# Another order for scores and weighted values in the steps that carry no block of projections

## The chip, the cores and the metric

The kernel runs on one core of one Trainium2 chip. The metric is the device time of one launch in microseconds (us). A figure for "before" is the median of its timed runs; a profile comes from one further execution, whose own time is given beside it.

## What is computed

Two attention blocks, A and B, run over the same 2048 tokens of 640 features, with 32 heads of 20 features each and with weights of their own. A sigmoid gate mixes their outputs token by token. Cut to what matters:

```
def block(x, wqkv, wo):                       # x: 1 x 2048 x 640
    q, k, v = split(x @ wqkv)                 # 32 heads, Dh = 20
    p = softmax(q @ k.T * Dh ** -0.5)         # full 2048 x 2048, each head
    return (p @ v) @ wo

g = sigmoid((x * gate_w).sum(-1, keepdims=True))
return g * block(x, A_wqkv, A_wo) + (1 - g) * block(x, B_wqkv, B_wo)
```

## The kernel before

Four heads form a group, and each block has eight groups, so there are 16 in all (`2 * NG`). For each group the kernel walks over four blocks of 512 queries, and for each of these over eight pairs of key tiles of 128 keys. One such pair, for one query block and four heads, is a *step*: 16 x 4 x 8 = 512 steps (`STEPS`). A step `G` issues three kinds of TensorE work:

- eight **e** matmuls (line 672, in `scores`): scores of 128 keys against 512 queries for one head. ScalarE turns each into exponentials (line 675) and stores them in a buffer `pt`.
- up to eight **m** matmuls (line 614, in `max_mm`): scores of 128 queries against 512 keys for a later step's softmax maximum, some 15 steps ahead. Most are reduced on VectorE by one maximum (line 625). One in eight, in the groups of which this text speaks, goes to ScalarE instead (a ReLU, line 618), and VectorE joins it with another matmul's scores (line 622). So a full step gives ScalarE eight exponentials and one ReLU, and VectorE six maxima and one joined maximum.
- two **V**, the blocks of weighted values (line 690, in `values`): for 128 keys, four matmuls with the exponentials of four heads, which add into the tile `acc`. They use the exponentials of step `G - 1`.

An e or m matmul uses one half of TensorE's rows: heads with `j = 0` the partitions from 0 on, heads with `j = 1` those from 64 on. In the strings below, `e0` and `m0` stand for the first half, `e1` and `m1` for the second. Both kinds are called *scores* in this text. Each writes one of seven PSUM tiles (`bank`, `NB = 7`), and the tile is free again when ScalarE or VectorE has read it. `take` hands out the tiles while the program is written, by a running estimate of which comes free first. `acc` has a tile of its own.

Beside this the steps carry other TensorE work: *blocks*, written **X**, are pieces of the next groups' projections or of the output product (line 407). The function `slot` issues one. The rest of the step (DMAs, small tasks) is advanced once for each `e`.

The order in which a step's pieces are issued is written out by hand, in three strings, one for steps without a block, one for steps with one, and one for steps with two. Cut to its core, the loop is:

```
STEP = ("e0 m1 V e1 m0 e0 m1 e1 m0 e0 m1 e1 m0 V e0 m1 e1 m0",
        "X e0 m1 m0 e1 m0 m1 V m1 e0 e1 m0 e1 e0 V m0 e1 e0 m1",
        "X m0 m1 e0 m1 e0 e1 V e1 e0 m1 m0 V e1 m0 m1 m0 e0 e1 X")
...
        blocks = 0 if not current and not any(f[0] <= G for f in fill) else 2 if behind(G) else 1
        for what in (STEP[blocks] if maxima or some else ...).split():
            k = count[what] = count.get(what, 0) + 1
            if what[0] == "e":   # also: advance the small tasks
                scores(G, (k - 1) // 2, (k - 1) % 2, (int(what[1]),))
            elif what[0] == "m":
                for u, ch in some[(k - 1) * len(some) // 4:k * len(some) // 4]:
                    one_max(u, ch, int(what[1]))
            elif what == "V":
                values(G - 1, k - 1)
            else:
                slot(G)
```

TensorE, ScalarE and VectorE each take their instructions in the order of the program.

`STEP[0]` is used in 20 of the 512 steps: 60 to 65, 162 to 167, 184 and 185, 190 and 191, and the single steps 452, 459, 466 and 489. All 20 have their full eight m. The steps with one block are by far the most. In the text, V1 and V2 are the two V of a step, and *inner* is a pair of neighbouring steps that both use `STEP[0]`.

Of the kernel before, what the change touches and what calls it, by code (L numbers as in the profile page):

```python
# [50 lines left out]
OFINE = (16, 16, 6, 16)  # L51


STEP = ("e0 m1 V e1 m0 e0 m1 e1 m0 e0 m1 e1 m0 V e0 m1 e1 m0",
        "X e0 m1 m0 e1 m0 m1 V m1 e0 e1 m0 e1 e0 V m0 e1 e0 m1",
        "X m0 m1 e0 m1 e0 e1 V e1 e0 m1 m0 V e1 m0 m1 m0 e0 e1 X")
LATE = "e0 e1 e0 e1 V X e0 e1 e0 e1 V"
# [14 lines left out]
def kernel(  # L72
# [1100 lines left out]
    for G in range(STEPS + 1):  # L1173
# [12 lines left out]
        count = {}  # L1186
        for what in (STEP[blocks] if maxima or some else LATE + " X" * (blocks == 2)).split():
            k = count[what] = count.get(what, 0) + 1
# [58 lines left out]
```

## Time and profile before

| | |
|---|---|
| median of 3 runs | 2762.35 us (2762.08 to 2764.07) |
| the profiled execution's own time | 2762.97 us |
| its span, first to last instruction | 2761.2 us |
| granted TensorE clock, mean | 0.996 |
| PE (TensorE matmul) busy | 2722.8 us, 99% of the span |
| ACT (ScalarE) busy | 2528.5 us, 92% |
| DVE (VectorE) busy | 2444.3 us, 89% |
| POOL (GpSimd) busy | 667.0 us, 24% |

The views name an engine, a line of the kernel and the tiles (`out<-in`), with the count behind an x. In the view in order of time, a row gives start and length in us, and equal neighbours are merged into one row with their count. A V shows there as one row of eight matmuls, since each of its four shows twice. A busy share is that of an engine's spans, and the ends of matmuls are modelled, so that short waits of PE can lie hidden under it.

### The profile page before, as it was taken

To read this page: it belongs to the slowest core of one execution; us is meant where nothing else is said; L and a number is where in the kernel's file an instruction comes from. 1 tells how busy PE (TensorE), PEld (TensorE's weight loads), DVE (VectorE), ACT (ScalarE), POOL (GpSimd) and SP (SyncE) were. 2 spreads that over 40 slices of the span, in tenths; PEclk is the share of its full clock that TensorE was granted. 3 is DMA by queue.
4 is the path that set the end of the run, shared out by engine and by line. 5 is a ranking of instruction groups with operands and counts; after the bars stand their busy time and mean duration, and the time that the engine had idled before them with its cause. 6 is when DMAs were issued, how large, how long until landed. Compare 5 with 4: busy or idle time off the path is not lost.

```text
span 2761.2 us, 62247 instructions
## 1 busy us (share of the span) xinstructions
PE 2722.8 (99%) x23273; PEld 935.9 (34%) x23273; DVE 2444.3 (89%) x4785; ACT 2528.5 (92%) x5128; POOL 667.0 (24%) x909
## 2 busy tenths in 40 slices
PE   7999999999999999999999999999999999999998
PEld 3433333333333332333333333333333333333222
DVE  7789899999999989888888998989988898999982
ACT  4999999999999999999999999999999999999987
POOL 6232222222123421311221111222342202100111
PEclk8999999999999999999999999999999999999999
DMA  4021102010120211102012230221201112132112
GB/s 143 16 57 26 31 11 47 7 31 16 25 55 20 60 42 49 43 9 61 20 45 62 60 85 25 60 56 48 65 17 42 30 50 63 32 78 63 47 48 76
DMA packets 176432, 125.58 MB, mean 45 GB/s; under 512 B 105216, under 2 KB 145976, under 8 KB 176128
## 3 DMA queue, kind: packets, MB, share of 16 engines
q1 hardware_dynamic: 173584, 119.99, 17.1%
q8 instruction: 182, 2.98, 0.5%
q0 software_dynamic: 1600, 0.96, 0.2%
q14 instruction: 122, 1.00, 0.1%
q10 hardware_dynamic: 944, 0.66, 0.1%
HBM read 55.53 MB, written 31.86 MB: 32 GB/s over the span
## 4 chain that ended last, share of the span: by engine, by line
PE 94%; DVE 4%; ACT 1%; DMA 1%; issue 0%; POOL 0%; POOLq 0%; SPq 0%; ACTq 0%; DVEq 0%
PE acc L690 35%; PE bank L407 20%; PE bank L614 20%; PE bank L672 18%; DVE mpart L625 2%; ACT pt L675 1%; DMA ws<-in_A_wqkv_dram 0%; PE bank L854 0%; DVE rl L622 0%; PE bank L900 0%; DVE ot L777 0%; DMA xs<-in_A_x_dram 0%; POOL wstage L336 0%; ACT rl L618 0%; DVE es L216 0%
## 5 line engine op out<-in xcount | busy, mean ns | idle before, releaser
L675 ACT ACTIVATE pt<-bank 128x512 f32<-128x512 f32 x4096 | 2168.5, 613 | 146.0 <-PE bank L672 98.0
L625 DVE TENSOR_REDUCE mpart<-bank 128x1 f32<-128x512 f32 x2944 | 1843.7, 682 | 220.4 <-PE bank L614 118.8
L690 PE MATMUL acc<-pt,v 128*21 128x512 f32 x8192 | 1081.7, 600 | 1.4 <-DVE ot L777 1.2
L672 PE MATMUL bank<-qt,kt 64*128 64x512 f16 x4096 | 1041.7, 380 | 4.6 <-DVE mpart L625 2.9
L614 PE MATMUL bank<-kt,qt 60*128 60x512 f16 x3520 | 1011.6, 380 | 4.2 <-ACT pt L675 1.3
L614 PEld LDWEIGHTS <-qt 60*128 60x128 f16 x4096 | 238.4, 94 | 883.4 <-issue 821.9
L622 DVE CUSTOM_DVE_ANT_0 rl<-bank,rl 128x512 f32<-128x512 f32 x576 | 388.1, 680 | 7.0 <-ACT rl L618 2.2
L618 ACT ACTIVATE rl<-bank 128x512 f32<-128x512 f32 x576 | 336.9, 594 | 7.1 <-PE bank L614 6.7
L672 PEld LDWEIGHTS <-kt 64*128 64x128 f16 x4096 | 230.2, 94 | 199.4 <-issue 88.5
L690 PEld LDWEIGHTS acc<-pt,v 128*21 128x21 f32 x8192 | 143.0, 99 | 431.9 <-issue 426.4
L407 PE MATMUL bank<-xx,wbh 128*128 128x168 f16 (+3 forms) x2480 | 287.7, 236 | 1.4 <-DVE wbh L926 1.0
L407 PE MATMUL bank<-xx,wbl 128*128 128x168 f16 (+3 forms) x1240 | 257.5, 235 | 0.0
L785 POOL TENSOR_TENSOR ot<-ot,sq 128x512 f32<-128x512 f32 x63 | 66.0, 1048 | 755.3 <-DVE sq L782 755.3
L407 PEld LDWEIGHTS <-wbh 128*128 128x128 f16 x2480 | 192.8, 98 | 110.8 <-issue 104.5
L614 PE MATMUL bank<-kd,qt 60*128 60x512 f16 x576 | 203.7, 379 | 0.1
L407 PE MATMUL bank<-woh,o_in 128*128 128x320 f16 (+3 forms) x700 | 157.7, 290 | 0.0
L407 PE MATMUL bank<-wvh,xx 128*128 128x160 f16 (+1 forms) x1280 | 156.7, 234 | 0.6 <-DVE mpart L622 0.6
L436 POOL CAST cq<-fs 128x512 f16<-128x512 f32 x60 | 36.6, 610 | 477.3 <-ACT fs L434 473.6
L407 PEld LDWEIGHTS <-xx 128*128 128x128 f16 x1920 | 131.1, 97 | 59.1 <-issue 56.3
L407 PE MATMUL bank<-wvl,xx 128*128 128x160 f16 (+1 forms) x640 | 137.7, 232 | 0.0
L407 PEld LDWEIGHTS <-wbl 128*128 128x128 f16 x1240 | 121.1, 98 | 4.7 <-issue 1.3
L407 PEld LDWEIGHTS <-o_in 128*128 128x128 f16 (+1 forms) x1050 | 87.3, 97 | 90.7 <-issue 68.8
(145 smaller groups left out, 1247.4 us busy)
## 6 DMA issues: line engine op xcount, KB each, us to landing
y_scr<-y_out SPq DMA_DIRECT2D x48, 320.0 KB
y_out<-y_scr SPq DMA_DIRECT2D x32, 320.0 KB
kt<-cq SPq DMA_DIRECT2D x120, 80.0 KB
o_scr<-on SPq DMA_DIRECT2D x240, 40.0 KB
o_in<-o_scr SPq DMA_DIRECT2D x64, 96.0 KB
kt<-cq SPq DMA_DIRECT2D x136, 40.0 KB
wstage<-in_B_wqkv_dram SPq DMA_DIRECT2D x13, 400.0 KB
xs<-in_A_x_dram SPq DMA_DIRECT2D x8, 640.0 KB
```

What stands on the lines that cost most here:

```text
L407: nc.tensor.matmul(out_ap, a, b, start=(k == 0), stop=(k == len(pairs) - 1))
L436: nc.gpsimd.tensor_copy(hi, f)
L614: nc.tensor.matmul(pt, QT[g % 2][r, pair, q0:q0 + P], k, start=True, stop=True)
L618: nc.scalar.activation(relus[u, j], pt, AF.Relu)
L622: nc.vector.tensor_tensor_reduce(rl, pt, rl, 1.0, LOW, OP.add, OP.max, m)
L625: nc.vector.tensor_reduce(m, pt, axis=AX.X, op=OP.max)
L672: nc.tensor.matmul(et, KT[g % 2][r, pair, kt * P:(kt + 1) * P], QT[g % 2][r, pair, qb * QB:(qb + 1) * QB], start=True, stop=True)
L675: nc.scalar.activation(pt, et, AF.Exp, scale=factor(g // 4))
L690: nc.tensor.matmul(acc[32 * h:32 * h + VW, :], V[(g // 2) % 2][:, kt, (g % 2) * GH + h, :], ptiles.pop((G, kk, h)), start=(kt == 0), stop= ...
L785: nc.gpsimd.tensor_tensor(t3, t3, sq.unsqueeze(2).to_broadcast([P, 16, 32]), op=OP.mult)
```

## The change

Only the first string changes. It holds the same pieces in the same numbers (four each of e0, e1, m0 and m1, and two V).

```
-STEP = ("e0 m1 V e1 m0 e0 m1 e1 m0 e0 m1 e1 m0 V e0 m1 e1 m0",
+STEP = ("e0 m0 m1 V m0 e1 e1 m0 m1 e1 e0 V e0 m1 m1 e0 e1 m0",
         "X e0 m1 m0 e1 m0 m1 V m1 e0 e1 m0 e1 e0 V m0 e1 e0 m1",
```

The instructions of PE, DVE and ACT are moved within the 20 steps, and from the first of them on the scores' PSUM tiles carry other numbers. Apart from those numbers, nothing else in the order of these three engines differs, and on POOL and SP the order is the same throughout.

First place: PE, the beginning of step 60, from its first e to just behind its first V. L672 is an e, L614 an m (`kd` and `kt` are keys, `qt` queries), and the row of L690 is the V. Before:

```order
L672 LDWEIGHTS kt_83
L672 MATMUL bank_90<-qt_81,kt_83 128x512
L614 LDWEIGHTS qt_80
L614 MATMUL bank_89<-kt_82,qt_80 128x512
L690 MATMUL acc<-pt,v_86 21x512 x4
L672 LDWEIGHTS kt_83
L672 MATMUL bank_93<-qt_81,kt_83 128x512
```

The same place in the changed kernel:

```order
L672 LDWEIGHTS kt_83
L672 MATMUL bank_90<-qt_81,kt_83 128x512
L614 LDWEIGHTS qt_80
L614 MATMUL bank_89<-kd_84,qt_80 128x512
L614 LDWEIGHTS qt_80
L614 MATMUL bank_93<-kt_82,qt_80 128x512
L690 MATMUL acc<-pt,v_86 21x512 x4
L614 LDWEIGHTS qt_80
L614 MATMUL bank_94<-kt_82,qt_80 128x512
```

One more score stands ahead of V1: the m on `kd`, which came behind it before. Of the three, the first two are e0 and m0, on the same half of the rows.

Second place: ACT, the nine instructions of step 60, eight exponentials (L675) and one ReLU (L618). Before:

```order
L675 ACTIVATE pt<-bank_90 128x512
L675 ACTIVATE pt<-bank_93 128x512
L618 ACTIVATE rl<-bank_94 128x512
L675 ACTIVATE pt<-bank_91 128x512
L675 ACTIVATE pt<-bank_95 128x512
L675 ACTIVATE pt<-bank_89 128x512
L675 ACTIVATE pt<-bank_92 128x512
L675 ACTIVATE pt<-bank_90 128x512
L675 ACTIVATE pt<-bank_95 128x512
```

And in the changed kernel:

```order
L675 ACTIVATE pt<-bank_90 128x512
L618 ACTIVATE rl<-bank_89 128x512
L675 ACTIVATE pt<-bank_91 128x512
L675 ACTIVATE pt<-bank_92 128x512
L675 ACTIVATE pt<-bank_93 128x512
L675 ACTIVATE pt<-bank_89 128x512
L675 ACTIVATE pt<-bank_91 128x512
L675 ACTIVATE pt<-bank_95 128x512
L675 ACTIVATE pt<-bank_93 128x512
```

The ReLU comes one place earlier. Before, one of these nine belongs to a score ahead of V1, six to scores between V1 and V2, and two to scores behind V2; now it is two, four and three.

## The prediction

> **What bounds the kernel now.** I read the page's busy table and its chain first, then one run of six neighbouring steps with the first string as a whole, then PE in order of time inside that run. The busy table and the chain, shares of the span:
>
> ```profile
> PE 2722.8 (99%) x23273; PEld 935.9 (34%) x23273; DVE 2444.3 (89%) x4785; ACT 2528.5 (92%) x5128; POOL 667.0 (24%) x909
> ...
> PE 94%; DVE 4%; ACT 1%; DMA 1%; issue 0%; POOL 0%; POOLq 0%; SPq 0%; ACTq 0%; DVEq 0%
> ```
>
> By these, TensorE is all that counts. But the change touches 20 steps of 512, so they must be read by themselves. The six steps 162 to 167 lie between 921 and 954 us; the view by windows gives the busy time of PE, PEld, DVE, ACT and POOL there:
>
> ```profile
> 921.00:954.00 33.00, 32.10 (x234) 7.95 (x231) 31.07 (x60) 31.42 (x63) 18.42 (x20) 1.00 0.29 62
> ```
>
> Here ACT is busy for 95% of the time and DVE for 94%, more than over the whole kernel, and PE for 97%. Three engines are close to full, so what counts is who waits for whom. PE in order of time, from the V2 of step 164 (937.82) over the V1 of step 165 (939.56) to its V2 (942.41):
>
> ```profile
> 937.82 1.05 PE L690 MATMUL acc<-pt,v 128*21 128x512 f32 x8
> 938.81 0.39 PE L672 MATMUL bank<-qt,kt 64*128 64x512 f16 x1
> 938.81 0.60 PE L614 MATMUL bank<-kt,qt 60*128 60x512 f16 x2
> 939.04 0.59 PE L672 MATMUL bank<-qt,kt 64*128 64x512 f16 x2
> 939.26 0.38 PE L614 MATMUL bank<-kt,qt 60*128 60x512 f16 x1
> 939.56 1.05 PE L690 MATMUL acc<-pt,v 128*21 128x512 f32 x8
> 940.55 0.39 PE L672 MATMUL bank<-qt,kt 64*128 64x512 f16 x1
> 940.55 0.39 PE L614 MATMUL bank<-kd,qt 60*128 60x512 f16 x1
> 940.78 0.38 PE L614 MATMUL bank<-kt,qt 60*128 60x512 f16 x1
> 940.78 0.59 PE L672 MATMUL bank<-qt,kt 64*128 64x512 f16 x2
> 941.00 0.38 PE L614 MATMUL bank<-kt,qt 60*128 60x512 f16 x1
> 941.22 0.38 PE L672 MATMUL bank<-qt,kt 64*128 64x512 f16 x1
> 941.62 0.37 PE L614 MATMUL bank<-kt,qt 60*128 60x512 f16 x1
> 941.97 0.37 PE L672 MATMUL bank<-qt,kt 64*128 64x512 f16 x1
> 942.11 0.37 PE L614 MATMUL bank<-kt,qt 60*128 60x512 f16 x1
> 942.41 1.05 PE L690 MATMUL acc<-pt,v 128*21 128x512 f32 x8
> ```
>
> Four lengths can be read off. A V holds the next score back by 0.99 us (939.56 to 940.55). Two scores on different halves start together (940.55), and the next pair follows 0.22 later (940.78, 941.00, 941.22): I call 0.22 a *pitch*. A V starts 0.30 after the last score (942.11 to 942.41). And the stretch from V1 to V2, ten scores or five pitches' worth, takes 2.85 where 0.99 + 4 x 0.22 + 0.30 = 2.17 would do. Its first seven scores go at the pitch; the eighth, at 941.62, comes 0.40 after the seventh, and the rest go one by one. The other stretch, from V2 to V1 with six scores, takes 1.74 and has no wait.
>
> Why the eighth waits is seen on ACT in the same stretch:
>
> ```profile
> 940.98 0.60 ACT L675 ACTIVATE pt<-bank 128x512 f32<-128x512 f32 x1
> ...
> 941.47 0.59 ACT L618 ACTIVATE rl<-bank 128x512 f32<-128x512 f32 x1
> 941.95 0.60 ACT L675 ACTIVATE pt<-bank 128x512 f32<-128x512 f32 x1
> ```
>
> There are seven tiles for scores. The first exponential begins 0.43 after its score (940.55 to 940.98), takes 0.60 and ends at 941.58; 0.04 later, at 941.62, the eighth score starts. It has waited for this tile. Ten scores between two V are more than seven tiles carry, and six are fewer; while PE is in a V, ACT and DVE have only the left-over scores to live on.
>
> ACT's own pitch is 0.48 (941.47 to 941.95), so its nine instructions need at least 9 x 0.48 = 4.32 us a step. DVE's pitch is that of a row of four maxima with no gap inside (window on DVE):
>
> ```profile
> 1209.38 2.48 DVE L625 TENSOR_REDUCE mpart<-bank 128x1 f32<-128x512 f32 x4 [0.48 <-PE bank L614]
> ```
>
> (2.48 - 0.68) / 3 = 0.60, with the single one's 0.68 from the group below; six of them and one joined maximum, 0.68, make 4.28 us:
>
> ```profile
> L625 DVE TENSOR_REDUCE mpart<-bank 128x1 f32<-128x512 f32 x2944 | 1843.7, 682 | 220.4 <-PE bank L614 118.8
> L622 DVE CUSTOM_DVE_ANT_0 rl<-bank,rl 128x512 f32<-128x512 f32 x576 | 388.1, 680 | 7.0 <-ACT rl L618 2.2
> ```
>
> An inner step takes 1.74 + 2.85 = 4.59 now. Neither engine's floor explains that: about 0.27 a step is bad order.
>
> **The change part by part.** The new string has three scores ahead of V1, seven between V1 and V2, and six behind V2. Nothing is added or taken away, no DMA changes its place in SP's or POOL's queue, and V2 still finds its four exponentials one whole step old. So all is in three kinds of stretch.
>
> *V1 to V2, 20 times.* Seven scores fit into seven tiles. On the halves they read 0 1, 1 0, 1, 1 0: four pitches with one half-empty, so 0.99 + 3 x 0.22 + 0.30 = 1.95 us. That the first seven after a V go without a wait is what the rows from 940.55 to 941.22 show. Against 2.85 this is -0.90, times 20: **-18.0**. I cost all twenty at 2.85. The first and the last of the twenty, and the one of step 162, in order:
>
> ```profile
> 408.80 1.06 PE L690 MATMUL acc<-pt,v 128*21 128x512 f32 x8
> 411.65 1.06 PE L690 MATMUL acc<-pt,v 128*21 128x512 f32 x8
> ...
> 923.14 1.06 PE L690 MATMUL acc<-pt,v 128*21 128x512 f32 x8
> 924.88 1.06 PE L690 MATMUL acc<-pt,v 128*21 128x512 f32 x8
> 928.30 1.06 PE L690 MATMUL acc<-pt,v 128*21 128x512 f32 x8
> ...
> 2634.71 1.06 PE L690 MATMUL acc<-pt,v 128*21 128x512 f32 x8 [0.20 <-DVE ot L777]
> 2637.63 1.06 PE L690 MATMUL acc<-pt,v 128*21 128x512 f32 x8
> ```
>
> They take 2.85, 3.42 and 2.92, and all twenty together 60.4, which is 3.4 over 20 x 2.85. I take that surplus to be other VectorE work that falls into such a stretch, and leave it in: it is worth -3.4 if the freer tiles swallow it, and nothing if not.
>
> *V2 to V1, 12 times inside a run.* Now nine scores follow each other: six, then e0 m0 m1 of the next step. On the halves: 0 1, 1 0, 1 0, 0, 0 1. That is five pitches, 0.99 + 4 x 0.22 + 0.30 = 2.17 without a wait. But the eighth has to wait for a tile again. The first exponential behind V2 frees one at 0.99 + 0.43 + 0.60 + 0.04 = 2.06, later than the eighth's place at 0.99 + 0.88 = 1.87. The ninth waits for the first maximum, 0.99 + 0.43 + 0.68 + 0.04 = 2.14, and V1 comes at 2.44. Against 1.74 that is +0.70, times 12: **+8.4**. An inner step is then 1.95 + 2.44 = 4.39 instead of 4.59, just over ACT's 4.32 and DVE's 4.28, so both can follow. The ends are 2.37, which with 1.95 makes ACT's floor, and 2.85, what ten scores take now.
>
> *Into a run, 8 times.* Three scores stand ahead of V1 where there were two, and e0 and m0 share a half: one pitch, +0.22. Ahead of step 162 (923.14 to 924.88, 1.74) nothing waits today, so the floor is near; if the third score has to wait for one more exponential, it is 0.22 + 0.48 = 0.70. I take +0.30: **+2.4**.
>
> *Out of a run, 8 times.* Behind the last V2 stand six scores in place of four, +0.22, and one exponential and one maximum more are left over for the next step. That step begins with a block, which covers them in part, as at step 452, a single one:
>
> ```profile
> 2451.71 1.06 PE L690 MATMUL acc<-pt,v 128*21 128x512 f32 x8
> ...
> 2453.24 0.27 PE L407 MATMUL bank<-woh,o_in 128*128 128x216 f16 x1
> ...
> 2454.18 0.39 PE L672 MATMUL bank<-qt,kt 64*128 64x512 f16 x1
> ```
>
> The block holds PE for 0.94 (2453.24 to 2454.18), in which ACT and DVE can do one such extra each; but they are behind already when it starts. The ends are +0.22 and 0.22 + 0.60 = +0.82 (a whole maximum uncovered). I take +0.42, a third of the way, since the block covers the larger part: **+3.4**.
>
> The sum is -18.0 + 8.4 + 2.4 + 3.4 = **-3.8 us** on the profiled execution's 2762.97, which gives 2759.2. The median of the runs is 0.6 lower, so I forecast 2758.6.
>
> **A rule that speaks against it.** The string puts same-half scores beside each other (e0 m0, e1 e1 later on). The rows at 940.55 show that different halves start together, and those at 940.78 and 941.00 that one half takes a new score each 0.22. The Trainium skill, "TensorEngine Tiling (Array Packing)", Key Properties, says that different tiles of the array can load weights and multiply in parallel, which makes alternating halves the good order. By that rule alone, with TensorE as the bound, only lost pitches would count. The trace agrees with the rule, but not with the bound: 0.68 of the 2.85 is waiting, three times a pitch.
>
> **The rivals.** About 0.2%, 5.5 us, is what I take a measurement of this kernel to tell from no change.
>
> - *More gain* (chance 0.18). The surplus of 3.4 goes too, entries and exits cost their floor of 0.22 (-0.6 and -1.6), and inner steps reach ACT's 4.32 (12 x -0.07 = -0.8): -10.2, 2752.1. For it: DVE idles beside PE's waits. Against it: surplus VectorE work must be done in any case.
> - *All comes back* (0.14). ACT and DVE are at 95% and 94%, so the time gained between V1 and V2 returns as waits for tiles: 0.90 a step in each inner V2 to V1 (10.8) and 0.45 in each entry and exit (7.2): 0, 2762.4. Against it: the floors of 4.32 and 4.28 lie below 4.59.
> - *Only pitches count* (0.04). The sixteen scores take eight pitches now (1 ahead of V1, 5 between, 2 behind) and nine in the new string (2, 4 and 3), as pairs on one half share none. One pitch more, 0.22, in 20 steps with every wait as it is: +4.4, 2766.8. Against it: the waits hang on the ten scores that are gone.
> - *Slower* (0.06). Nine scores run out of tiles as the ten do today. V2 to V1 then takes 2.85 in inner steps (12 x 1.11 = 13.3), entries and exits cost their upper ends (8 x 0.70 = 5.6, 8 x 0.82 = 6.6): +7.5, 2769.9. With such entries and exits, an inner V2 to V1 over 2.68 is what makes it more than 5.5 us. For it: the stretch is only one score shorter than the one that waits now. Against it: two of its nine scores wait by the rows, not three.
>
> **How the numbers follow.** The forecast, -3.8 or thereabouts, has the remaining 0.58. It is a difference of large terms, 18.0 against 14.2, so its own ends (-5.5 to -1) come from an error of 0.1 us in an inner stretch and 0.1 in an exit. The range of 8 in 10 takes in half of the way to the larger gain and most of the case in which all comes back, and leaves out the last two rivals and the full gain: 2755.0 to 2763.0. Faster by over 0.2% is the first rival alone, 0.18; slower the last, 0.06; the forecast and the other two lie within 0.2%, 0.76.
>
> **What would show it.** In the changed profile, V1 to V2 in the run of 162 to 167 should be near 1.95 with no gap among its seven scores, V2 to V1 near 2.44 with the wait at the eighth score, and a whole inner step near 4.39. Step 452's stretch from V2 (2451.71, above) to the next V1, in the row below, is 3.22 and should grow to about 3.6:
>
> ```profile
> 2454.93 1.06 PE L690 MATMUL acc<-pt,v 128*21 128x512 f32 x8
> ```
>
> Outside the 20 steps and the one behind each, nothing should move. It would be wrong if the seven scores wait between V1 and V2, if inner V2 to V1 comes to 2.68 or more, or if steps far from the 20 change because tiles are handed out in another rotation.

## The result, and the profile after

| | before | after |
|---|---|---|
| median of 22 runs each | 2762.86 us (2762.07 to 2764.49) | 2759.18 us (2758.43 to 2761.13) |
| profiled execution's own time | 2762.97 us | 2761.0 us |
| its span | 2761.2 us | 2759.2 us |

The ratio is 0.9987, with a 95% interval of 0.9982 to 0.9993: 3.7 us or 0.13% faster. The interval leaves out 1, and the gain is within the 0.2% that the prediction counted as no change. The forecast was -3.8 us (2758.6).

PE in order of time in the changed kernel, from the V2 of step 164 (936.44) over the V1 of step 165 (938.94) to its V2 (940.90), the same place as in the prediction:

```profile
936.44 1.06 PE L690 MATMUL acc<-pt,v 128*21 128x512 f32 x8
937.43 0.39 PE L672 MATMUL bank<-qt,kt 64*128 64x512 f16 x1
937.44 0.39 PE L614 MATMUL bank<-kt,qt 60*128 60x512 f16 x1
937.66 0.38 PE L672 MATMUL bank<-qt,kt 64*128 64x512 f16 x1
937.66 0.59 PE L614 MATMUL bank<-kt,qt 60*128 60x512 f16 x2
937.88 0.59 PE L672 MATMUL bank<-qt,kt 64*128 64x512 f16 x2
938.54 0.37 PE L614 MATMUL bank<-kd,qt 60*128 60x512 f16 x1
938.63 0.37 PE L614 MATMUL bank<-kt,qt 60*128 60x512 f16 x1
938.94 1.05 PE L690 MATMUL acc<-pt,v 128*21 128x512 f32 x8
939.92 0.39 PE L614 MATMUL bank<-kt,qt 60*128 60x512 f16 x1
939.93 0.39 PE L672 MATMUL bank<-qt,kt 64*128 64x512 f16 x1
940.15 0.38 PE L614 MATMUL bank<-kt,qt 60*128 60x512 f16 x1
940.15 0.38 PE L672 MATMUL bank<-qt,kt 64*128 64x512 f16 x1
940.37 0.38 PE L614 MATMUL bank<-kt,qt 60*128 60x512 f16 x1
940.50 0.46 PE L672 MATMUL bank<-qt,kt 64*128 64x512 f16 x2
940.90 1.06 PE L690 MATMUL acc<-pt,v 128*21 128x512 f32 x8
```

V1 to V2 takes 1.96 us (2.85 before): its seven scores take no more than the four pitches that they need (the row at 940.50 joins the last two, of which the second starts at 940.59). V2 to V1 takes 2.50 (1.74 before): seven scores at the pitch, then a hole up to the eighth at 938.54. An inner step takes 4.46 where it took 4.59 (4.39 forecast). What the eighth and the ninth wait for stands on ACT and DVE. A pair of exponentials on ACT, then one maximum on DVE:

```profile
937.38 1.11 ACT L675 ACTIVATE pt<-bank 128x512 f32<-128x512 f32 x2
```

```profile
937.89 0.69 DVE L625 TENSOR_REDUCE mpart<-bank 128x1 f32<-128x512 f32 x1
```

The second of the exponentials is the one of the first score behind V2. It ends at 937.38 + 1.11 = 938.49, and the eighth score starts at 938.54; the maximum ends at 938.58, and the ninth starts at 938.63.

The run of 162 to 167 by windows, with the busy times of PE, PEld, DVE, ACT and POOL (the window ends 1 us earlier than the one before, as the run does):

```profile
921.00:953.00 32.00, 31.62 (x237) 8.72 (x237) 31.01 (x59) 31.14 (x64) 18.19 (x19) 1.00 0.30 63
```

ACT is busy for 97% of it and DVE for 97%, where it was 95% and 94%. The starts of the V in all 20 steps give the terms of the prediction's sum (sums over the steps named, from one profiled execution of each kernel):

| stretch | before | after | difference | predicted |
|---|---|---|---|---|
| V1 to V2, 20 times | 60.44 | 41.10 | -19.3 | -18.0 |
| V2 to V1 inside a run, 12 | 23.35 | 33.03 | +9.7 | +8.4 |
| into a run, 8 | 14.83 | 17.18 | +2.4 | +2.4 |
| out of a run, 8 | 27.80 | 31.27 | +3.5 | +3.4 |
| sum | 126.42 | 122.58 | -3.8 | -3.8 |

The two profiled executions differ by 2.0 us only, since the stretches before the first V, between the other steps and behind the last V are 0.4, 0.4 and 1.0 us longer in this execution of the changed kernel. The first lies ahead of every moved instruction, so it is no effect of the change, and the last is 0.1 us shorter than before in the run with alternating halves in this schedule (below), so that one varies too. In the middle part, the largest changes are +0.3, +0.2 and +0.1 us in the steps just behind a run (186, 490 and 467) and -0.3 in step 316, which is far from any. The first three look like an effect that reaches one step further than the table; with one execution of each kernel that is not shown. Its 22 runs spread over 2.7 us. The median is the measure of the whole, and the trace that of the parts.

### The profile page after: what moved, and what is told of

The parts are those of the page before. It is cut to its first block, busy times and chain, and to the rows that moved or that the text cites. A ratio compares the mean times of both kernels' runs of the same rounds, so it can differ in the third digit from the quotient of the medians.

```text
span 2759.2 us, 62203 instructions
## 1 busy us (share of the span) xinstructions
PE 2722.9 (99%) x23273; PEld 940.3 (34%) x23273; DVE 2443.9 (89%) x4785; ACT 2528.0 (92%) x5128; POOL 666.7 (24%) x909
## 4 chain that ended last, share of the span: by engine, by line
PE 94%; DVE 3%; ACT 1%; DMA 1%; issue 0%; POOL 0%; POOLq 0%; SPq 0%; ACTq 0%; DVEq 0%
PE acc L690 35%; PE bank L407 20%; PE bank L614 20%; PE bank L672 18%; DVE mpart L625 2%; ACT pt L675 1%; DMA ws<-in_A_wqkv_dram 0%; PE bank L854 0%; DVE rl L622 0%; PE bank L900 0%; DMA xs<-in_A_x_dram 0%; DVE ot L777 0%; DVE es L216 0%; ACT rl L618 0%; PE bank L829 0%
## 5 line engine op out<-in xcount | busy, mean ns | idle before, releaser
L675 ACT ACTIVATE pt<-bank 128x512 f32<-128x512 f32 x4096 | 2166.9, 613 | 143.0 <-PE bank L672 101.4
L690 PE MATMUL acc<-pt,v 128*21 128x512 f32 x8192 | 1081.9, 600 | 0.1
L672 PE MATMUL bank<-qt,kt 64*128 64x512 f16 x4096 | 1038.1, 380 | 2.4 <-DVE mpart L625 1.3
L614 PE MATMUL bank<-kt,qt 60*128 60x512 f16 x3520 | 1008.5, 381 | 4.1 <-ACT pt L675 1.5
L614 PEld LDWEIGHTS <-qt 60*128 60x128 f16 x4096 | 238.9, 94 | 900.3 <-issue 833.0
L618 ACT ACTIVATE rl<-bank 128x512 f32<-128x512 f32 x576 | 338.1, 596 | 7.4 <-PE bank L614 7.0
L672 PEld LDWEIGHTS <-kt 64*128 64x128 f16 x4096 | 230.6, 95 | 176.7 <-issue 66.5
L690 PEld LDWEIGHTS acc<-pt,v 128*21 128x21 f32 x8192 | 143.7, 99 | 431.3 <-issue 426.6
L614 PE MATMUL bank<-kd,qt 60*128 60x512 f16 x576 | 203.6, 379 | 1.3 <-DVE mpart L622 0.5
```

Of the source, the lines that this page charges most:

```text
L614: nc.tensor.matmul(pt, QT[g % 2][r, pair, q0:q0 + P], k, start=True, stop=True)
L618: nc.scalar.activation(relus[u, j], pt, AF.Relu)
L672: nc.tensor.matmul(et, KT[g % 2][r, pair, kt * P:(kt + 1) * P], QT[g % 2][r, pair, qb * QB:(qb + 1) * QB], start=True, stop=True)
L675: nc.scalar.activation(pt, et, AF.Exp, scale=factor(g // 4))
L690: nc.tensor.matmul(acc[32 * h:32 * h + VW, :], V[(g // 2) % 2][:, kt, (g % 2) * GH + h, :], ptiles.pop((G, kk, h)), start=(kt == 0), stop= ...
```

## The experiments

In the kernel's own schedule the change is worth 3.7 us, too little to tell theories apart by their size. So a schedule was made that uses the first string 13 times as often: of each eight steps, four get two blocks each and four none. In it 260 steps use the string, in 63 runs with 197 inner pairs.

**Old and new string, used 260 times.** The edit of both, and the text on record for each:

```
         blocks = 0 if not current and not any(f[0] <= G for f in fill) else 2 if behind(G) else 1
+        if blocks and G < 496:
+            blocks = 2 if G % 8 < 4 else 0
```

> The old string, in a schedule that uses it 13 times as often: of each eight steps the first four get two blocks each and the last four none, as far as there are blocks. It is then used in 260 steps, in 63 runs, with 197 inner pairs. This is the base for the others of this set. All theories: slower than the kernel before, as the four steps in a row without a block leave TensorE waiting for ScalarE and VectorE (4.59 us a step), and the two-block steps are longer than TensorE's mean; inner steps should take 4.59 as before, V1 to V2 2.85, V2 to V1 1.74.

> The same schedule with the new string. Theory (the count of scores between two V against seven PSUM tiles decides): the four terms as they were measured in the change, 260 x -0.97 (V1 to V2) + 197 x 0.81 (inner V2 to V1) + 63 x 0.30 (into a run) + 63 x 0.43 (out of a run) = -46 us against the old string in this schedule. Rival 1 (only the pitches of the halves count): 260 x 0.22 = +57 us. Rival 2 (ScalarE and VectorE are the bound, and what is gained comes back): 0 within 10 us.

Measured: 2897.16 us with the old string and 2852.83 with the new one (ratios to the kernel before 1.0485, interval 1.0467 to 1.0502, and 1.0323, 1.0306 to 1.0340). The new string is 44.3 us faster, 46 were expected; rivals 1 and 2 gave +57 and 0. A row for each V of neighbouring steps, V1 first, old string and then new:

```profile
1732.69 1.06 PE L690 MATMUL acc<-pt,v 128*21 128x512 f32 x8
1735.54 1.06 PE L690 MATMUL acc<-pt,v 128*21 128x512 f32 x8
1737.28 1.06 PE L690 MATMUL acc<-pt,v 128*21 128x512 f32 x8
```

```profile
1706.78 1.06 PE L690 MATMUL acc<-pt,v 128*21 128x512 f32 x8
1708.74 1.06 PE L690 MATMUL acc<-pt,v 128*21 128x512 f32 x8
1711.24 1.06 PE L690 MATMUL acc<-pt,v 128*21 128x512 f32 x8
```

2.85 and 1.74 against 1.96 and 2.50: to 0.01 us the stretches of the kernel's own 20 steps. By the two traces, the four kinds of stretch add up to -44.1 us (-234.1, +156.7, +14.1 and +19.2), and all the rest differs by 0.5. So the gain is one of the string and grows with its use; it doesn't come from other steps, where only the rotation of the tiles is new.

**Eight and eight.** The first string becomes the one in the text on record.

> The same schedule, with eight scores between V1 and V2 and eight between V2 and V1, halves strictly alternating (eight pitches a step, the fewest there can be): e0 m1 V e1 m0 e0 m1 e1 m0 e0 m1 V e1 m0 e0 m1 e1 m0. Theory (tiles): in both stretches the eighth score waits for the first exponential behind the V, so each takes 0.99 + 0.43 + 0.60 + 0.04 + 0.30 = 2.36 and an inner step 4.72, more than with the old string (4.59): 260 x (2.36 - 2.85) + 197 x (2.36 - 1.74) + 63 x 0.30 = +14 us against the old string in this schedule, that is about 60 us slower than the new one. Rival (an even split feeds ScalarE and VectorE best, and no pitch is lost): at least as fast as the new string, with inner steps at ScalarE's 4.32, some -55 us against the old.

Measured: 2929.69 us (1.0603, 1.0585 to 1.0621), 32.5 us slower than the old string and 77 slower than the new. The rival is refuted: the even split without a lost pitch is the slowest of the three. The theory had the sign, and less than half of the size. PE in an inner step, from a V2 (1752.48) over the next V1 (1754.93) to its V2 (1757.36):

```profile
1752.48 1.06 PE L690 MATMUL acc<-pt,v 128*21 128x512 f32 x8
1753.47 0.39 PE L672 MATMUL bank<-qt,kt 64*128 64x512 f16 x1
1753.47 0.60 PE L614 MATMUL bank<-kt,qt 60*128 60x512 f16 x2
1753.70 0.59 PE L672 MATMUL bank<-qt,kt 64*128 64x512 f16 x2
1753.92 0.38 PE L614 MATMUL bank<-kt,qt 60*128 60x512 f16 x1
1754.14 0.38 PE L672 MATMUL bank<-qt,kt 64*128 64x512 f16 x1
1754.62 0.37 PE L614 MATMUL bank<-kt,qt 60*128 60x512 f16 x1
1754.93 1.06 PE L690 MATMUL acc<-pt,v 128*21 128x512 f32 x8
...
1757.36 1.05 PE L690 MATMUL acc<-pt,v 128*21 128x512 f32 x8
```

The eighth score alone is late: it starts 1754.62 - 1752.48 = 2.14 behind the V, where 2.06 was expected. It does wait for the first exponential, as the theory has it, but this one comes later. ACT, the exponential of the score at 1753.47:

```profile
1753.96 0.62 ACT L675 ACTIVATE pt<-bank 128x512 f32<-128x512 f32 x1
```

It begins 0.49 behind its score and not 0.43, and ends at 1754.58, 0.04 ahead of the eighth score. In 438 of the 459 stretches of this run with eight scores and no block, the trace puts the end of the eighth's wait down to an exponential. Why it begins later here is open. The stretches from V1 to V2 and from V2 to V1 are then 2.43 and 2.45 here, where 2.36 was expected of both: over 260 and 197 of them that is 18 + 18 = 36 us. Half of it was taken back, as the old string's stretches in this schedule are on average 2.90 and 1.77 and not 2.85 and 1.74 (means over all 260 and 197).

**The new counts with alternating halves.** Only the order within the stretches differs from the new string.

> The same schedule, with the new string's counts (three scores ahead of V1, seven between, six behind) but with the halves alternating as far as odd counts let them: e0 m1 m0 V e1 m0 e1 e0 m1 e1 m0 V e0 m1 m0 e1 e0 m1. Theory (counts and tiles): the same as the new string, within 5 us. Rival (neighbours on the same half are a price that the new string pays): faster than the new string by up to 0.22 x 260 = 57 us.

Measured: 2851.05 us (1.0319, 1.0302 to 1.0336), 1.8 us faster than the new string in this schedule, within the 5 of the theory and far from the rival's 57. But the rival's price was set too high: seven scores take four pitches and nine take five in whichever order, so both strings have nine pitches a step, and there was no lost pitch to win back. What this run shows is that at equal pitches it hardly counts which halves are neighbours. That a lost pitch doesn't decide is shown by eight and eight, which has eight pitches a step and is 77 us slower. The same was tried in the kernel's own schedule:

> The kernel's own schedule (20 steps) with the new string's counts, three, seven and six, but halves alternating as far as they can. Theory (counts decide, not which halves are neighbours): -3.7 us against the kernel before, as the change, within 1 us. Rival (the change pays for neighbours on one half): up to 4.4 us faster than the change, about -8.

Measured: 2759.61 us against 2762.12 of the kernel before (0.9991, interval 0.9982 to 1.0000), -2.5 us. The four terms of its trace add up to -3.7 (-19.3, +9.7, +2.3 and +3.6), as the change's do to -3.8. The median misses the expected -3.7 by 1.2 us, 0.2 more than was allowed for; the intervals of the two strings overlap, and I read no difference between them. It is not the rival's -8, which rests on the same price as its 57.

**One tile fewer.** In the steps that use the first string, scores get six PSUM tiles instead of seven. Old and new string, both in the schedule with 260 uses:

```
-    now = [-1]
+    now, few = [-1], [0]
...
-        i = min((k for k in range(NB) if k not in held), key=lambda k: free_at[k])
+        i = min((k for k in range(NB - few[0]) if k not in held), key=lambda k: free_at[k])
...
-        count = {}
+        count, few[0] = {}, 1 if not blocks and maxima else 0
```

> The old string in the schedule that uses it 260 times, with one PSUM tile fewer (six) handed out to scores in just these steps. Theory (tiles decide): in the ten scores between V1 and V2 the seventh waits already, so that V1 to V2 grows from 2.85 by 0.2 to 0.4; the six scores from V2 to V1 still fit, 1.74 in inner steps. In all 50 to 110 us slower than with seven tiles. Rival (ScalarE and VectorE are the bound by their throughput, and tiles only pass the wait on): within 10 us of seven tiles.

> The same with the new string. Theory (tiles decide): seven scores no longer fit. Between V1 and V2 the seventh waits for the first exponential, 2.06 + 0.30 = 2.36 instead of 1.96; from V2 to V1 the ninth waits for the second exponential (about 0.99 + 0.43 + 0.48 + 0.63 + 0.04 = 2.57), 2.87 instead of 2.49: 260 x 0.40 + 197 x 0.38 = +180 us against seven tiles, and with six tiles the new string has lost its advantage over the old one. Rival (throughput): within 10 us of seven tiles, and still some 45 us faster than the old string.

Measured: 3010.08 us with the old string (1.0898, 1.0881 to 1.0915) and 3032.86 with the new (1.0978, 1.0961 to 1.0995). Against seven tiles that is +113 (50 to 110 expected, so a little over the range) and +180 (180 expected); the kernel before, run beside each set, took 2763.63 us beside the seven tiles and 2762.12 beside the six. The new string has not only lost its lead, it is 23 us behind. V1, V2 and the next V1 with six tiles, old string:

```profile
1804.96 1.06 PE L690 MATMUL acc<-pt,v 128*21 128x512 f32 x8
1808.27 1.06 PE L690 MATMUL acc<-pt,v 128*21 128x512 f32 x8
1810.02 1.06 PE L690 MATMUL acc<-pt,v 128*21 128x512 f32 x8
```

Its six scores still fit into six tiles, and V2 to V1 stays at 1.75; the ten wait longer, 3.31 (3.05 to 3.25 expected). The new string over one step, V1 at 1819.20:

```profile
1819.20 1.06 PE L690 MATMUL acc<-pt,v 128*21 128x512 f32 x8
...
1820.86 0.81 PE L672 MATMUL bank<-qt,kt 64*128 64x512 f16 x2
1821.60 1.06 PE L690 MATMUL acc<-pt,v 128*21 128x512 f32 x8
...
1823.73 0.37 PE L672 MATMUL bank<-qt,kt 64*128 64x512 f16 x1 [0.32 <-ACT pt L675]
1823.94 0.38 PE L614 MATMUL bank<-kd,qt 60*128 60x512 f16 x1
1824.22 0.37 PE L614 MATMUL bank<-kt,qt 60*128 60x512 f16 x1
1824.52 1.06 PE L690 MATMUL acc<-pt,v 128*21 128x512 f32 x8
```

V1 to V2 is 2.40, since the seventh score (the second in the row at 1820.86) now has to wait, and V2 to V1 is 2.92. The text on record gave 2.36 and 2.87. The row at 1823.73 is the seventh score behind V2, and names what ended its wait: an exponential. The instructions and their order per engine are those of the run with seven tiles, only the tiles' numbers differ; so the tiles are what decides here, and not the engines' throughput. The Trainium skill, "TensorEngine Tiling (Array Packing)", PSUM Bottleneck, says that tiling speeds up TensorE but not the evacuation of PSUM. These runs agree: behind a V, TensorE starts seven scores within 0.66 us when there are seven tiles, and with six the seventh starts only when a reader has freed a tile.

None of these runs points to an order that would beat the changed kernel by more than can be measured.

## Why the prediction was right, point by point

- *The bound.* That the ten scores between V1 and V2 run out of seven tiles was the basis of all terms. The runs with six tiles show it: a stretch with as many scores as tiles has no wait, one with more waits at the first score over.
- *V1 to V2.* 1.95 was predicted and 1.96 measured in most of the 20. Of the surplus of 3.4 us, which the prediction put down to other VectorE work, 1.9 is still there (41.10 less 20 x 1.96). The prediction had left it in whole, so this term came out 1.3 us better than forecast.
- *V2 to V1 inside a run.* 2.44 predicted, 2.50 measured, with the waits at the eighth and the ninth score for the exponential and the maximum that were named. The exponential ended 1.06 behind its score (937.43 to 938.49) and not 1.03, and the maximum 1.14 (937.44 to 938.58) and not 1.11. The term came out 1.3 us larger than forecast; 0.06 in each of 12 stretches is 0.7 of it. The rest is surplus: these stretches had 2.5 us of it before (23.35 less 12 x 1.74), which the prediction did not mention, and have 3.0 now (33.03 less 12 x 2.50). Part of what V1 to V2 lost stands here. In step 62, V1 to V2 went from 3.34 to 1.96 and V2 to V1 from 1.75 to 3.02, and the last of a chain of small VectorE operations, which stood between V1 (417.99) and V2 (421.33) before, stands behind V2 (420.33) now:

```profile
420.56 0.31 DVE L239 COPY wrow<-es 64x1 f32<-64x1 f32 x2
```

```profile
421.46 0.31 DVE L239 COPY wrow<-es 64x1 f32<-64x1 f32 x2
```

That the two errors, -1.3 and +1.3, cancel so well is luck: the forecast had neither.
- *Into a run.* +0.30 each was chosen close to the floor of 0.22, and the mean is +0.29. Single ones differ more than that: step 162 went from 1.74 to 2.12, step 452 from 2.12 to 2.14, since it had a wait already (its last score starts 1.82 behind the V before and 1.83 after).
- *Out of a run.* +0.42 each was a choice a third of the way between two ends, and +0.43 was measured. It was luck as much as reading. Step 452 went from 3.22 to 3.69, where 3.6 was expected. Its V1, V2 and next V1 in the changed kernel, with the last two scores ahead of the latter, and behind it the same two scores before the change:

```profile
2446.28 1.06 PE L690 MATMUL acc<-pt,v 128*21 128x512 f32 x8
...
2448.24 1.06 PE L690 MATMUL acc<-pt,v 128*21 128x512 f32 x8
...
2451.37 0.63 PE L614 MATMUL bank<-kt,qt 60*128 60x512 f16 x2
2451.93 1.06 PE L690 MATMUL acc<-pt,v 128*21 128x512 f32 x8
```

```profile
2454.62 0.38 PE L614 MATMUL bank<-kt,qt 60*128 60x512 f16 x2
```

The two m span 0.63 where they took 0.38 before: the last score ahead of the next V1 waits for its tile, so the block does not hide in full what is left over behind V2, as the prediction assumed. What the step behind a run takes after this stretch had no price in the sum; by the +0.3, +0.2 and +0.1 us above, it may have cost another 0.7.
- *The rivals.* "Only pitches count" and "all comes back" are refuted by the sets of 260 steps (+57 and 0 against the -44.3 measured), and the first of them also by eight and eight, where fewer pitches took longer. "Slower", nine scores that wait like ten, had its threshold at 2.68 for V2 to V1, and 2.50 was measured. "More gain" needed exits at their floor, and they were twice that.
- *The ends of the forecast.* The -5.5 to -1 do not follow from the errors named for them: 0.1 us in each of 12 inner stretches and 8 exits is 2.0, which gives -5.8 to -1.8. The result lies within either.

## What to carry to other kernels

Where one engine fills a fixed number of buffers in bursts and is held up in between, count the buffers' uses from one hold-up to the next: in these runs a burst no longer than the number of buffers had no wait, as a rule, and the first use beyond it waited for the first reader's whole latency (some 1.1 us from the start of its score), the next ones only for the next readers. So seven and nine beat eight and eight by 77 us in the same schedule, since the first has one stretch that waits and the second two. A sum of four terms read from one run of steps in the trace (lengths between fixed points, times counts from the order of the program) came within 0.1 us of the 3.7 measured, but by errors of 1.3 us in two terms that cancelled; so an error of about 1 us would have been no surprise.

## What was not expected of the hardware

A high busy share of PE says nothing of such waits. With six tiles and the new string the page reads:

```profile
PE 2915.4 (96%) x23273; PEld 975.2 (32%) x23273; DVE 2481.2 (82%) x4785; ACT 2540.8 (84%) x5128; POOL 666.4 (22%) x909
```

That is 96%, although its inner steps take 5.32 us where the pitches alone make 1.95 + 2.17 = 4.12: a score's row is 0.37 to 0.39 us long and the pitch 0.22, so a wait of under some 0.15 us hides behind the row before. The Trainium skill, "Perfetto Trace Analysis", Identifying the Most-Contended Engine, says that matmul busy time is not a good measure of how close a kernel is to its roofline. These rows agree, by the overlap of 0.15 us between neighbours.
